# Linear attention and two FFNs on one core: another order of the first FFN's slots, its first sum in two parts, and z written over r

## The chip, the core and the metric

The kernel runs on one core of a Trainium2 chip. The metric is the device time of one execution in microseconds (us), as the median of several runs; lower is better. The core's engines are TensorE (PE, whose weight loads are listed apart as PEld), VectorE (DVE), ScalarE (ACT), GpSimd (POOL) and SyncE (SP), which issues most DMA transfers. The "granted clock" is the share of full speed that the chip allowed TensorE; its two levels are 1.2 and 2.4 GHz.

## The reference

```python
# r, k, v, w: (4, 8, 768, 48); u: (8, 48)
for t in range(S):
    cur = einsum('bhd,bhe->bhde', u * k_t, v_t)
    y[:, :, t] = einsum('bhd,bhde->bhe', r_t, state + cur)
    state = w_t[..., None] * state + einsum('bhd,bhe->bhde', k_t, v_t)
x = y.transpose(0, 2, 1, 3).reshape(3072, 384)
# first FFN, d_ff 2048
h = x @ w_in
x = (h * clip(h + 3, 0, 6) / 6) @ w_out
# second FFN, d_ff 1024
h = x @ w_in2
solu = h * softmax(h)
out = (layernorm(solu) * g_ln) @ w_out2
```

The four FFN weights arrive as 64-bit floats, which the kernel has to turn into pairs of 32-bit numbers itself.

## The kernel before, in words

**Tiles and groups.** The 768 steps of a sequence are cut into 6 groups of 128; a group of the 4 batch entries is 4 tiles, so there are 24 tiles, and tile i belongs to group i // 4. A group is 512 tokens wide (GT), and the first FFN works on whole groups.

**Attention.** A tile passes five stages, `stages = [stw, st0, st1, st2, st3]`. `stw` clamps w on POOL. `st0` transposes w and r on PE into PSUM (wt, rt; from tile 10 on DVE does this from another layout, `late`), and DVE makes running products with eight scans (four into q, four into e) and multiplies e by rt. `st1` transposes k (kt), multiplies q by kt on DVE, and makes z = r*k*u on POOL, in a buffer of its own. `st2` transposes q back (ktp), multiplies q and e on PE into pa0 and pa1, reduces z to d on DVE, and masks on POOL (`am`, a multiplication) and DVE (`am`, a predicated copy from pa0 and pa1). `st3` makes kv and the output yt on PE; DVE adds kv into the state (s_st, twice a tile), ACT copies yt to xh, and DVE makes the remainder xl = yt - xh. All of wt, rt, kt, ktp, pa0, pa1, kv and yt are tiles of one PSUM pool, `ps_a`, with 3 buffers. The state ties tile i to tile i + 4; a group's FFN needs xh and xl of its four tiles.

**The first FFN.** It runs in 96 slots; slot n is (g, m) = divmod(n, 16), chunk m of 128 hidden units for group g. Every product is three matmuls of high and low parts. `ffn_in(n)` runs 9 matmuls into h (2 PSUM buffers), then ACT `t` (L639), DVE `t` (L640), ACT `gh` (L641) and `gl` (L643), on POOL in the first 16 slots and on DVE later. `ffn_out(n - 2)` runs 9 matmuls into the group's three accumulators y (three PSUM banks, one set), in PSUM over all 16 chunks; after the last ACT copies them to `ye` and stores them to `y1d` in DRAM (L661, L662). `xp` holds xh and xl with 2 buffers, and `ye` takes a buffer of xl.

**Weights.** Chunk m of the first FFN's weights is loaded raw by SP (`w1_load`, four DMAs, 2 buffers `raw`), decoded by `w1_a` (DVE L40 and L43, ACT L44) and by `w1_b` (DVE L50 and L53, ACT L60 for w_h, DVE L61 for w_l). L53 is the last to read the raw buffer.

**The order.** A prologue computes the four tiles of group 0 and decodes chunks 0 to 2. Then the program loops over n = 0 to 97: `ffn_in(n)`, the attention stages that the table `sched` puts at n, `ffn_out(n - 2)`, and in slots 0 to 12 the second half of chunk n + 3's decode, the first half of chunk n + 4's and the load of chunk n + 5. Tile i from 4 on has its last stage at slot 4(i - 4) + 2, so tiles 4 to 11 are finished at slots 2, 6, ... 30. In these loops the order of an engine's instructions is arranged by the framework's scheduler, so an engine's rows needn't stand in the order of the program. After slot 78 (NA) the weights of the second FFN are decoded, and after slot 97 the second FFN runs, tile by tile.

Of the kernel before, what the change touches and what calls it, by code (L numbers as in the profile page):

```python
# [8 lines left out]
F32 = mybir.dt.float32  # L9
# [258 lines left out]
def fast_path(  # L268
# [52 lines left out]
    ffp = left.enter_context(tc.tile_pool(name="ff", bufs=3, side="left"))  # L321
    xp = left.enter_context(tc.tile_pool(name="x", bufs=2, side="left"))
    ps_h = left.enter_context(tc.tile_pool(name="ps_h", bufs=2, space=PSUM, side="left"))
# [173 lines left out]
    def st1(i):  # L497
# [20 lines left out]
        nc.vector.tensor_tensor(out=q[0:DP, :, 1:C + 1], in0=kt[0:DP], in1=q[0:DP, :, 1:C + 1], op=ALU.mult)  # L518
        z = atp.tile([P, H, D], F32, tag="z", name="z", bufs=1)
        nc.gpsimd.tensor_tensor(out=z, in0=a["r"][:, :, 0:D], in1=a["k"][:, :, 0:D], op=ALU.mult)  # L520
        nc.gpsimd.tensor_tensor(out=z, in0=z, in1=u_bc, op=ALU.mult)
# [34 lines left out]
    def st3(i):  # L556
# [51 lines left out]
        if b == 0:  # L608
            x_t[g] = (
                xp.tile([P, KD, GT], F32R, tag="xh", name="xh"),  # L610
                xp.tile([P, KD, GT], F32R, tag="xl", name="xl"),
            )
        xh, xl = x_t[g]
# [11 lines left out]
    def ffn_in(n):  # L625
        g, m = divmod(n, M1)
        xh, xl = x_t[g]
# [13 lines left out]
        nc.scalar.activation(out=gh, in_=t, func=ACTF.Copy)  # L641
        eng = nc.gpsimd if n < M1 else nc.vector
        eng.tensor_tensor(out=gl, in0=t, in1=gh.bitcast(F32), op=ALU.subtract)  # L643
        g_t[n] = (gh, gl)

    def ffn_out(n):
        g, m = divmod(n, M1)
        if m == 0:
            y_ps[g] = [ps_y.tile([P, GT], F32, tag=f"y{c}", name=f"y{c}") for c in range(KD)]
        gh, gl = g_t.pop(n)  # L650
        for c in range(KD):
            cs = slice((KD + c) * P, (KD + c + 1) * P)
            wh, wl = w1_h[:, m, cs], w1_l[:, m, cs]
            for j, (a, b) in enumerate([(wh, gh), (wh, gl), (wl, gh)]):
                nc.tensor.matmul(  # L655
                    out=y_ps[g][c], lhsT=a, rhs=b, start=(m == 0 and j == 0), stop=(m == M1 - 1 and j == 2)
                )
        if m == M1 - 1:
            ye = xp.tile([P, KD, GT], F32, tag="xl", name="ye")
            for c in range(KD):  # L660
                nc.scalar.activation(out=ye[:, c, :], in_=y_ps[g][c], func=ACTF.Copy, scale=1.0 / 6.0)  # L661
                nc.scalar.dma_start(out=y1d[g, :, c, :], in_=ye[:, c, :])  # L662
            del y_ps[g]

# [97 lines left out]
    order.close()  # L762
    NA = 4 * (NTILE - B - 1) + 2
    sched = {}
    for i in range(B, NTILE):
        for s in range(NS):
            sched.setdefault(4 * (i - B) + (s - 3 if s < NS - 1 else 2), []).append((i, s))
    for n in sorted(q for q in sched if q < 0):
# [4 lines left out]
    for n in range(NSLOT + LAG):  # L773
# [8 lines left out]
        if n >= LAG:  # L782
            ffn_out(n - LAG)
        if n + LD < M1:
            w1_b(n + LD)
        if n + LD + 1 < M1:
            w1_a(n + LD + 1)
        if n + LD + 2 < M1:
            w1_load(n + LD + 2)
        if n == M1:  # L790
            dec_st.close()
            late_open()
# [125 lines left out]
```

## Time and profile before

| | us |
|---|---|
| runs | 800.91, 800.93, 802.08 (median 800.93) |
| profiled execution | 802.91 |
| its span, first to last instruction | 801.2 |
| mean granted clock of TensorE | 0.970 |
| PE busy in the span | 759.3 (95%) |
| DVE busy | 542.5 (68%) |
| ACT busy | 332.1 (41%) |
| POOL busy | 263.1 (33%) |

The rows further down come from the profiled execution. "Busy" is the time in which an engine has an instruction running. In a row of single instructions the first number is the start and the second the duration in us, and a bracket at the end says how long the engine was idle before it and what ended the wait; "xN" joins N like instructions. L numbers are lines of the kernel before.

### The profile page before, as it was taken

Reading aid. Unit: us, or ns where it says so; the run is one execution under the profiler, and the core shown is the slowest. Engines: PE = TensorE matmul, PEld = TensorE weight load, DVE = VectorE, ACT = ScalarE, POOL = GpSimd, SP = SyncE. Lnnn points to the kernel's source line nnn. Section 1 sums busy time; section 2 is a strip of 40 time slices with the busy share of each in tenths; the row PEclk is TensorE's granted clock in tenths of the full one; section 3 lists DMA queues with packets and bytes.
Section 4 is the critical chain, followed back from the end, with each engine's and each line's share of the span. In section 5 each row is a group of like instructions: output and inputs, shape, how many; then the busy total and the mean of one; then the engine's idle time right before and its main releaser. Section 6 shows DMA issues by size and latency. Waiting matters only on the chain. (4 is left out here: it accounts for less than half of the span.)

```text
span 801.2 us, 13241 instructions
## 1 busy us (share of the span) xinstructions
PE 759.3 (95%) x4922; PEld 639.5 (80%) x4922; DVE 542.5 (68%) x1037; ACT 332.1 (41%) x615; POOL 263.1 (33%) x356
## 2 busy tenths in 40 slices
PE   5788987899999999999999999999999999999996
PEld 4566766688888888888888888877889999999996
DVE  5879789866777776667767665898375555555552
ACT  3355444342334444343344333654353344443342
POOL 5488225573333333333332230232122222222210
PEclk9688889999999999999999999999999999999999
DMA  9964564344333433343323202431111111111001
GB/s 160 174 138 105 130 147 107 86 115 96 82 83 82 121 82 82 83 121 72 73 56 100 52 22 78 138 119 40 50 39 50 41 41 46 44 40 50 29 20 35
DMA packets 139433, 64.76 MB, mean 81 GB/s; under 512 B 90848, under 2 KB 133984, under 8 KB 139360
## 3 DMA queue, kind: packets, MB, share of 16 engines
q1 hardware_dynamic: 136768, 59.11, 31.4%
q10 hardware_dynamic: 2592, 4.72, 1.6%
q8 instruction: 41, 0.67, 0.4%
q14 instruction: 32, 0.26, 0.1%
HBM read 54.37 MB, written 9.44 MB: 80 GB/s over the span
## 5 line engine op out<-in xcount | busy, mean ns | idle before, releaser
L639 ACT ACTIVATE t<-h,three 128x512 f32<-128x512 f32 x96 | 65.8, 685 | 187.0 <-PE h L635 184.4
L635 PE MATMUL h<-xh,w_l 128*128 128x512 f32 x288 | 115.9, 402 | 4.7 <-DVE w_l L61 4.6
L640 DVE SCALAR_TENSOR_TENSOR t<-t,h 128x512 f32<-128x512 f32 x96 | 65.3, 680 | 80.8 <-ACT t L639 80.7
L635 PE MATMUL h<-xh,w_h 128*128 128x512 f32 x288 | 115.3, 401 | 3.6 <-DVE t L640 2.0
L655 PE MATMUL y<-gh,w_h 128*128 128x512 f32 x288 | 117.9, 409 | 0.0
L635 PE MATMUL h<-xl,w_h 128*128 128x512 f32 x288 | 114.9, 399 | 0.0
L655 PE MATMUL y<-gl,w_h 128*128 128x512 f32 x288 | 113.6, 394 | 0.2 <-DVE gl L643 0.2
L655 PE MATMUL y<-gh,w_l 128*128 128x512 f32 x288 | 113.3, 393 | 0.0
L550 POOL TENSOR_TENSOR am<-ident,d 128x512 f32<-128x512 f32 x48 | 59.4, 1259 | 160.3 <-PE yt L585 158.0
L641 ACT ACTIVATE gh<-t 128x512 fp32r<-128x512 f32 x96 | 60.4, 630 | 52.8 <-DVE t L640 51.9
L643 DVE TENSOR_TENSOR gl<-t,gh 128x512 fp32r<-128x512 f32 x80 | 63.9, 798 | 21.8 <-ACT gh L641 21.6
L67 DVE TENSOR_REDUCE nm<-h 128x1 f32<-128x1024 f32 x24 | 29.4, 1225 | 62.6 <-PE h L827 62.5
L635 PEld LDWEIGHTS h<-xh,w_l 128*128 128x128 f32 x288 | 55.8, 194 | 17.9 <-DVE w_l L61 6.4
L635 PEld LDWEIGHTS h<-xh,w_h 128*128 128x128 f32 x288 | 55.2, 192 | 17.3 <-DVE t L640 3.6
L854 PE MATMUL po<-w_oh,qh 128*128 128x384 f32 x192 | 67.0, 349 | 0.3 <-ACT qh L843 0.3
L655 PEld LDWEIGHTS y<-gh,w_h 128*128 128x128 f32 x288 | 54.6, 190 | 15.3 <-ACT gh L641 1.8
L854 PE MATMUL po<-w_oh,ql 128*128 128x384 f32 x192 | 65.2, 339 | 0.1
L854 PE MATMUL po<-w_ol,qh 128*128 128x384 f32 x192 | 65.0, 339 | 0.0
L635 PEld LDWEIGHTS h<-xl,w_h 128*128 128x128 f32 x288 | 55.5, 193 | 11.7
L655 PEld LDWEIGHTS y<-gh,w_l 128*128 128x128 f32 x288 | 54.6, 190 | 12.1
L655 PEld LDWEIGHTS y<-gl,w_h 128*128 128x128 f32 x288 | 54.7, 190 | 11.0 <-DVE gl L643 0.9
L843 ACT ACTIVATE qh<-pt 128x512 fp32r<-128x512 f32 x48 | 26.1, 595 | 79.0 <-PE pt L841 79.0
(118 smaller groups left out, 1515.6 us busy)
## 6 DMA issues: line engine op xcount, KB each, us to landing
raw<-in_moe_w_out_dram SPq DMA_DIRECT2D x24, 384.0 KB
raw<-in_moe_w_in_dram SPq DMA_DIRECT2D x48, 128.0 KB
r<-in_r_dram SPq DMA_DIRECT2D x24, 192.0 KB
k<-in_k_dram SPq DMA_DIRECT2D x24, 192.0 KB
v<-in_v_dram SPq DMA_DIRECT2D x24, 192.0 KB
y1d<-ye ACTq DMA_DIRECT2D x18, 256.0 KB
y<-y1d SPq DMA_DIRECT2D x24, 192.0 KB
out_dram<-os SPq DMA_DIRECT2D x24, 192.0 KB
```

What stands on the lines that cost most here:

```text
L67: nc.vector.tensor_reduce(out=nm, in_=h, axis=AX.X, op=ALU.max, negate=True)
L550: nc.gpsimd.tensor_tensor(out=am, in0=ident.unsqueeze(1).to_broadcast([P, HP, C]), in1=dv[:, hh, :].unsqueeze(2).to_broadcast([P, HP, C]), ...
L635: nc.tensor.matmul(out=h, lhsT=a, rhs=b, start=(j == 0), stop=(j == len(ops) - 1))
L639: nc.scalar.activation(out=t, in_=h, func=ACTF.Relu, bias=three)
L640: nc.vector.scalar_tensor_tensor(out=t, in0=t, scalar=6.0, in1=h, op0=ALU.min, op1=ALU.mult)
L641: nc.scalar.activation(out=gh, in_=t, func=ACTF.Copy)
L643: eng.tensor_tensor(out=gl, in0=t, in1=gh.bitcast(F32), op=ALU.subtract)
L655: nc.tensor.matmul(out=y_ps[g][c], lhsT=a, rhs=b, start=(m == 0 and j == 0), stop=(m == M1 - 1 and j == 2))
L843: nc.scalar.activation(out=qh[:, ms, :], in_=pt, func=ACTF.Copy)
L854: nc.tensor.matmul(out=po, lhsT=x[:, m, :], rhs=y[:, m, :], start=(n == 0), stop=(n == 3 * M2 - 1))
```

## The change

The slots are listed in an order of their own: chunks 0 to 5 of group 0, then all 16 chunks of group 1, then chunks 6 to 15 of group 0, then groups 2 to 5 as before. So group 1 begins at slot 6, and its tiles 4 to 7 have their last stage at slots -1, 1, 3 and 5 (the first in the prologue); group 2 begins at slot 32 as before, and its tiles 8 to 11 end at slots 24, 26, 28 and 30. From tile 12 on the table is the same. Decodes of chunks 3 to 8 follow in slots 0 to 5, those of 9 to 15 in slots 6, 8, ... 18. Since there is one set of accumulators, group 0's sum leaves PSUM after its sixth chunk, by three ACT copies to `part`, and at its end three DVE operations add `part` to the rest. The buffers of x are named a and b in place of two turns of one name, so that group 0's stay while group 1 runs. `gl` stays on POOL up to slot 19, the `late` pool opens at slot 20 in place of 16, and z is written over r.

```diff
+    K0 = 6
+    DEC_END = 20
+    slots = [(0, m) for m in range(K0)] + [(1, m) for m in range(M1)] + [(0, m) for m in range(K0, M1)]
+    slots += [(g, m) for g in range(2, NG) for m in range(M1)]
...
-    xp = left.enter_context(tc.tile_pool(name="x", bufs=2, side="left"))
+    xp = left.enter_context(tc.tile_pool(name="x", bufs=1, side="left"))
+    part_st = ExitStack()
+    part = part_st.enter_context(tc.tile_pool(name="part", bufs=1, side="left")).tile([P, KD, GT], F32, name="part")
...
+    x_room = "ab" + "ba" * (NG // 2)
...
-        z = atp.tile([P, H, D], F32, tag="z", name="z", bufs=1)
-        nc.gpsimd.tensor_tensor(out=z, in0=a["r"][:, :, 0:D], in1=a["k"][:, :, 0:D], op=ALU.mult)
+        z = a["r"][:, :, 0:D]
+        nc.gpsimd.tensor_tensor(out=z, in0=z, in1=a["k"][:, :, 0:D], op=ALU.mult)
...
     def ffn_in(n):
-        g, m = divmod(n, M1)
+        g, m = slots[n]
...
-        eng = nc.gpsimd if n < M1 else nc.vector
+        eng = nc.gpsimd if n < DEC_END else nc.vector
...
     def ffn_out(n):
-        g, m = divmod(n, M1)
-        if m == 0:
+        g, m = slots[n]
+        first = m == 0 or (g == 0 and m == K0)
+        last = m == M1 - 1 or (g == 0 and m == K0 - 1)
+        if first:
...
-        if m == M1 - 1:
-            ye = xp.tile([P, KD, GT], F32, tag="xl", name="ye")
+        if not last:
+            return
+        ys = y_ps.pop(g)
+        if m < M1 - 1:
             for c in range(KD):
...
+                nc.scalar.activation(out=part[:, c, :], in_=ys[c], func=ACTF.Copy, scale=1.0 / 6.0)
+            return
+        ye = xp.tile([P, KD, GT], F32, tag="xl" + x_room[g], name="ye")
+        for c in range(KD):
+            if g == 0:
+                nc.vector.scalar_tensor_tensor(
+                    out=ye[:, c, :], in0=ys[c], scalar=1.0 / 6.0, in1=part[:, c, :], op0=ALU.mult, op1=ALU.add
+                )
...
-    NA = 4 * (NTILE - B - 1) + 2
+    final = {}
+    for i in range(B, NTILE):
+        g, b = divmod(i, B)
+        if g == 1:
+            final[i] = [-1, 1, 3, 5][b]
+        elif g == 2:
+            final[i] = [24, 26, 28, 30][b]
+        else:
+            final[i] = (g - 1) * M1 + 4 * b + 2
+    NA = final[NTILE - 1]
...
-            sched.setdefault(4 * (i - B) + (s - 3 if s < NS - 1 else 2), []).append((i, s))
+            back = NS - 1 - s if i // B < 3 or s == NS - 1 else NS - s
+            sched.setdefault(final[i] - back, []).append((i, s))
+    dec_at = {}
+    for m in range(LD, M1):
+        dec_at[m - LD if m < K0 + LD else K0 + 2 * (m - K0 - LD)] = m
...
-        if n + LD < M1:
-            w1_b(n + LD)
-        if n + LD + 1 < M1:
-            w1_a(n + LD + 1)
-        if n + LD + 2 < M1:
-            w1_load(n + LD + 2)
-        if n == M1:
+        if n in dec_at:
+            m = dec_at[n]
+            w1_b(m)
+            if m + 1 < M1:
+                w1_a(m + 1)
+            if m + 2 < M1:
+                w1_load(m + 2)
+        if n == DEC_END:
             dec_st.close()
             late_open()
```

In the changed kernel's rows the attention lines are numbered some 7 higher (L491 and L497 are the scans L484 and L490, L561 is am L554, L611 is s_st L604, L646 is t L640, L501 is the product with rt L494).

How the change moves DVE's instructions is seen at two places. The first is inside a tile of group 1. Before, from the am of tile 5, with the t of slots 5 and 6:

```order
L554 COPY_PREDICATED am<-causal,pa_923 128x512
L61 TENSOR_TENSOR w_l<-dec,w_h 128x768
L554 COPY_PREDICATED am<-causal,pa_924 128x512
L50 SCALAR_TENSOR_TENSOR dec<-dec,raw 128x768
L640 SCALAR_TENSOR_TENSOR t<-t,h 128x512
L53 SCALAR_TENSOR_TENSOR dec<-raw,dec 128x768
L40 TENSOR_SCALAR dec<-raw 128x768
L640 SCALAR_TENSOR_TENSOR t<-t,h 128x512
L43 TENSOR_SCALAR raw<-raw 128x768
L61 TENSOR_TENSOR w_l<-dec,w_h 128x768
L50 SCALAR_TENSOR_TENSOR dec<-dec,raw 128x768
L604 TENSOR_TENSOR s_st_117<-kv,sp 48x4x48
```

After the change, from the am of tile 6, with the t of slot 3 (and the scans and e of tile 7):

```order
L561 COPY_PREDICATED am<-causal,pa_959 128x512
L561 COPY_PREDICATED am<-causal,pa_960 128x512
L491 SCALAR_TENSOR_TENSOR q<-wt,ones 112x128 x4
L53 SCALAR_TENSOR_TENSOR dec<-raw,dec 128x768
L495 RECIPROCAL e<-q 112x4
L40 TENSOR_SCALAR dec<-raw 128x768
L497 SCALAR_TENSOR_TENSOR e<-wt,e,ones 112x127 x4
L61 TENSOR_TENSOR w_l<-dec,w_h 128x768
L501 TENSOR_TENSOR e<-rt,e 112x512
L43 TENSOR_SCALAR raw<-raw 128x768
L646 SCALAR_TENSOR_TENSOR t<-t,h 128x512
```

Before, decode steps and two t stand between a tile's am and its s_st, and the next tile's scans come later still; now the next tile's scans (tile 7) follow the am at once, and one t lies between am and s_st.

The second place is behind the tiles of group 1. Before, from the t of slot 10, with the end of tile 6 and the scans of tile 7 (s_st, xl, q):

```order
L640 SCALAR_TENSOR_TENSOR t<-t,h 128x512
L61 TENSOR_TENSOR w_l<-dec,w_h 128x768
L43 TENSOR_SCALAR raw<-raw 128x768
L604 TENSOR_TENSOR s_st_119<-kv,sp 48x4x48
L50 SCALAR_TENSOR_TENSOR dec<-dec,raw 128x768
L604 TENSOR_TENSOR s_st_119<-kv,sp 48x4x48
L53 SCALAR_TENSOR_TENSOR dec<-raw,dec 128x768
L40 TENSOR_SCALAR dec<-raw 128x768
L617 TENSOR_TENSOR xl<-yt,xh 128x3x128
L61 TENSOR_TENSOR w_l<-dec,w_h 128x768
L43 TENSOR_SCALAR raw<-raw 128x768
L484 SCALAR_TENSOR_TENSOR q<-wt,ones 112x128 x4
```

After the change, from the t of slot 6, the first of group 1:

```order
L646 SCALAR_TENSOR_TENSOR t<-t,h 128x512
L53 SCALAR_TENSOR_TENSOR dec<-raw,dec 128x768
L646 SCALAR_TENSOR_TENSOR t<-t,h 128x512
L40 TENSOR_SCALAR dec<-raw 128x768
L61 TENSOR_TENSOR w_l<-dec,w_h 128x768
L43 TENSOR_SCALAR raw<-raw 128x768
L491 SCALAR_TENSOR_TENSOR q<-wt,ones 112x128
L50 SCALAR_TENSOR_TENSOR dec<-dec,raw 128x768
L646 SCALAR_TENSOR_TENSOR t<-t,h 128x512
L53 SCALAR_TENSOR_TENSOR dec<-raw,dec 128x768
L40 TENSOR_SCALAR dec<-raw 128x768
L491 SCALAR_TENSOR_TENSOR q<-wt,ones 112x128
```

Where before the decode steps of three chunks share the row with a tile, there are now t and decode steps with single scans of tile 8; all decode steps of chunks 8 to 15 stand in this manner ahead of the t of slot 15.

## Rows read from the trace of the kernel before

**Rows 1.** Timeline of DVE: t of slots 0 and 14 (start, duration, then the instruction)

```profile
61.76 0.67 DVE L640 SCALAR_TENSOR_TENSOR t<-t,h 128x512 f32<-128x512 f32 x1
...
160.46 0.67 DVE L640 SCALAR_TENSOR_TENSOR t<-t,h 128x512 f32<-128x512 f32 x1
```

**Rows 2.** Windows: stretch, length, busy PE, PEld, DVE, ACT, POOL, PE clock, DMA share, GB/s

```profile
62.40:161.20 98.80, 84.32 (x584) 66.95 (x586) 86.83 (x131) 44.38 (x74) 48.32 (x47) 0.89 0.45 113
161.20:267.80 106.60, 106.60 (x824) 88.71 (x816) 71.95 (x139) 41.48 (x79) 41.46 (x54) 1.00 0.42 96
```

**Rows 3.** Waits of DVE and PE, 62.4 to 161.2: total us, times, longest us

```profile
DVE dec L40 <- DMA raw<-in_moe_w_out_dram: 8.7, 6, 2.8
DVE am L554 <- POOL am L550: 0.6, 2, 0.3
...
PE rt L439 <- issue: 8.3, 3, 3.0
```

**Rows 4.** Timeline of ACT: t of slots in PE's full stage

```profile
240.78 0.69 ACT L639 ACTIVATE t<-h,three 128x512 f32<-128x512 f32 x1 [3.77 <-PE h L635]
244.86 0.69 ACT L639 ACTIVATE t<-h,three 128x512 f32<-128x512 f32 x1 [2.00 <-PE h L635]
...
261.51 0.69 ACT L639 ACTIVATE t<-h,three 128x512 f32<-128x512 f32 x1 [3.79 <-PE h L635]
```

**Rows 5.** Lines of DVE, 62.4 to 161.2: count, busy us, mean ns, idle before

```profile
L50 DVE SCALAR_TENSOR_TENSOR dec<-dec,raw 128x768 int32<-128x768 int32 x13 | 14.8, 1136 | 0.0
L53 DVE SCALAR_TENSOR_TENSOR dec<-raw,dec 128x768 int32<-128x768 int32 x13 | 14.6, 1123 | 0.0
L61 DVE TENSOR_TENSOR w_l<-dec,w_h 128x768 fp32r<-128x768 f32 x12 | 14.2, 1181 | 1.8 <-ACT w_h L60 1.7
L640 DVE SCALAR_TENSOR_TENSOR t<-t,h 128x512 f32<-128x512 f32 x15 | 10.1, 674 | 0.2 <-ACT t L639 0.2
L40 DVE TENSOR_SCALAR dec<-raw 128x768 f32<-128x768 f32 x12 | 9.3, 779 | 8.8 <-DMA raw<-in_moe_w_out_dram 8.7
L43 DVE TENSOR_SCALAR raw<-raw 128x768 int32<-128x768 int32 x12 | 6.9, 579 | 0.0
L490 DVE TENSOR_TENSOR_SCAN e<-wt,e,ones 112x127 f32<-112x127 f32 x12 | 4.8, 461 | 0.0
L484 DVE TENSOR_TENSOR_SCAN q<-wt,ones 112x128 f32<-112x128 f32 x12 | 4.1, 403 | 0.0
L494 DVE TENSOR_TENSOR e<-rt,e 112x512 f32<-112x512 f32 x4 | 2.7, 681 | 0.0
L604 DVE TENSOR_TENSOR s_st<-kv,sp 48x192 f32<-48x192 f32 x7 | 2.4, 348 | 0.1
L617 DVE TENSOR_TENSOR xl<-yt,xh 128x384 fp32r<-128x384 f32 x3 | 1.7, 558 | 0.1
L539 DVE TENSOR_REDUCE d<-z 128x8 f32<-128x384 f32 x2 | 1.1, 544 | 0.0
L488 DVE RECIPROCAL e<-q 112x4 f32<-112x4 f32 x3 | 0.5, 176 | 0.0
```

**Rows 6.** L61's durations over the span (min/median/max), and POOL's gl, 62.4 to 161.2

```profile
L61 DVE TENSOR_TENSOR w_l<-dec,w_h x16: 932/950/2028, 28.8 to 161.5; 128x768 fp32r<-128x768 f32 x16
...
L643 POOL TENSOR_TENSOR gl<-t,gh 128x512 fp32r<-128x512 f32 x14 | 20.3, 1452 | 29.1 <-ACT gh L641 29.1
```

**Rows 7.** Timeline of DVE and SP's queue: end of L53, load, L40

```profile
129.00 1.18 DVE L53 SCALAR_TENSOR_TENSOR dec<-raw,dec 128x768 int32<-128x768 int32 x1
...
130.21 1.16 SPq L353 DMA_DIRECT2D raw<-in_moe_w_in_dram  x2
...
137.66 0.56 DVE L40 TENSOR_SCALAR dec<-raw 128x768 f32<-128x768 f32 x1 [0.66 <-DMA raw<-in_moe_w_out_dram]
```

**Rows 8.** Timeline of PE behind slot 14's t

```profile
163.54 0.60 PE L439 MATMUL rt<-ident,r 128*112 128x128 f32 x4
...
169.24 0.39 PE L635 MATMUL h<-xh,w_h 128*128 128x512 f32 x1
```

More of the change, by code (lines that the diff above doesn't have):

```diff
@@ L608, in st3 @@
         if b == 0:
[L609 to L612, printed above, removed]
+            x_t[g] = [
+                xp.tile([P, KD, GT], F32R, tag=nm + x_room[g], name=nm) for nm in ("xh", "xl")
+            ]
         xh, xl = x_t[g]
@@ L655, in ffn_out @@
                 nc.tensor.matmul(
-                    out=y_ps[g][c], lhsT=a, rhs=b, start=(m == 0 and j == 0), stop=(m == M1 - 1 and j == 2)
+                    out=y_ps[g][c], lhsT=a, rhs=b, start=(first and j == 0), stop=(last and j == 2)
                 )
-        if m == M1 - 1:
-            ye = xp.tile([P, KD, GT], F32, tag="xl", name="ye")
+        if not last:
+            return
+        ys = y_ps.pop(g)
+        if m < M1 - 1:
             for c in range(KD):
-                nc.scalar.activation(out=ye[:, c, :], in_=y_ps[g][c], func=ACTF.Copy, scale=1.0 / 6.0)
-                nc.scalar.dma_start(out=y1d[g, :, c, :], in_=ye[:, c, :])
-            del y_ps[g]
+                nc.scalar.activation(out=part[:, c, :], in_=ys[c], func=ACTF.Copy, scale=1.0 / 6.0)
[7 more added lines that the diff above has]
+            else:
+                nc.scalar.activation(out=ye[:, c, :], in_=ys[c], func=ACTF.Copy, scale=1.0 / 6.0)
+            nc.scalar.dma_start(out=y1d[g, :, c, :], in_=ye[:, c, :])
+        if g == 0:
+            part_st.close()
     def range_flag():
@@ L762, in fast_path @@
     order.close()
-    NA = 4 * (NTILE - B - 1) + 2
+    final = {}
[5 more added lines that the diff above has]
+            final[i] = [24, 26, 28, 30][b]
+        else:
+            final[i] = (g - 1) * M1 + 4 * b + 2
+    NA = final[NTILE - 1]
     sched = {}
```

## Prediction

> **What bounds the kernel now.** I read the busy time of each engine by stage first, then what DVE and PE wait for in the stage where neither is full, then DVE's operations there. The profiled execution of before took 802.91 us for a span of 801.2 us; the runs have a median of 800.93 us, 2.0 us less, and I carry every difference over to that median unchanged. I cut the first FFN at two DVE operations that exist in both kernels: the t (L640) of slot 0, which ends at 62.43 us, and that of slot 14, which ends at 161.13 us [rows 1]. Between them PE works 84.32 of 98.80 us at a granted clock of 0.89, DVE 86.83; from there to slot 34's t, at 267.8 us, PE works 106.60 of 106.60 us at 1.00 [rows 2]. So up to slot 14 DVE with its waits sets the pace, and after it PE does. DVE's idle time in the first stage is 98.80 - 86.83 = 12.0 us, and 8.7 of it are waits of L40 for raw weights [rows 2, 3]. PE waits 8.3 us in three places for "issue" ahead of rt [rows 3]; rt takes one of the three buffers of ps_a, which wt, rt, kt, ktp, pa0, pa1, kv and yt share, so this is a wait for a buffer that DVE (or ACT) has yet to read.
>
> From tile 12 on both kernels have the same order, so all that the change can win or lose lies ahead of about slot 34. A slot without attention takes PE 4.08 us; four slots and one tile take 20.73 us, so a tile is 20.73 - 4 x 4.08 = 4.4 us of PE [rows 4].
>
> **The change, part by part.** *Until slot 0's t.* The new DVE row has one L50 and one L494 more ahead of it and one L539 less: 1.136 + 0.681 - 0.544 = 1.27 us of nominal durations [rows 5]. DVE operations overlap a little in the trace: the thirteen lines shown add up to 87.2 us and the two left out, q (L518) and am (L554), to 7.8; together they cover 86.83, a factor of 0.914 [rows 2, 5]. I take **+1.2 us**.
>
> *DVE's work from slot 0's t to slot 14's.* Decoding doesn't move out of the way: although the program now asks for one chunk in two slots, the rows of DVE after the change have all sixteen chunks ahead of slot 15's t, as before. Added are eight scans (four L490, four L484), two s_st, one xl, one reduction (and a reciprocal that is shorter than any of these); gone are one L50, one L53 and one L494. That is 4 x 0.461 + 4 x 0.403 + 2 x 0.348 + 0.558 + 0.544 + 0.18 - 1.136 - 1.123 - 0.681 = 2.5 us, times 0.914: **+2.3 us** [rows 5].
>
> *DVE's idle time there.* In the new order tiles 5, 6 and 7 go through DVE within five slots, where each used to have four, and after tile 7 there is no attention but a few scans until slot 15. So I price two legs.
> In the first leg a tile has nothing between its am and the next tile's scans but a decode step or two, so its chain through the three ps_a buffers and POOL is open. Below: 0.6 us, all that DVE waits for POOL's am now. Above: 8.3 us, if PE's three waits ahead of rt pass to DVE whole [rows 3]. I take the middle, 4.4 us, which is also three times one gl on POOL (1.452 us), the operation that POOL most likely has ahead of an am [rows 6]. With one wait for raw weights of 0.7 us [rows 7] the leg idles 5.1 us.
> In the second leg, from tile 7's xl to slot 14's t, the row holds 8 L50, 7 L53, 7 L61, 7 L40, 7 L43, 9 t, 8 scans and a reciprocal, 44.4 us nominal, times 0.914: 40.6 us [rows 5]. The loads give another bound. A raw buffer is refilled when L53 of its chunk ends: L53 ended at 130.18, the load left at 130.21, and L40 of the chunk two further on could start at 137.66, after a wait, 7.4 us later [rows 7]. From there to the end of that chunk's L53 the row has L40, L43, L61, a scan, L50, a t and L53: 5.88 x 0.914 = 5.4 us. Two buffers thus yield two chunks in 12.8 us, or with a scan less 12.4, so 6.3 us a chunk. Seven chunks are 44.1 us; L50 and L53 of chunk 8 stand ahead (+2.1), L53 of chunk 15 stands behind slot 14's t (-1.0): 45.2 us, of which 4.6 are idle. PE needs only 9 x 4.08 = 36.7 us for the nine slots there.
> Both legs idle 9.7 us where before had 12.0: **-2.3 us**. Slot 14's t thus ends at +1.2 + 2.3 - 2.3 = +1.2 us, at 162.3 us.
>
> *What PE has done by then.* Before, when slot 14's t ended at 161.13, PE still had the end of tile 7's yt, tile 8's wt, 27 FFN matmuls and tile 8's rt and kt to do until it came to h of slot 16 at 169.24: 8.1 us behind [rows 8]. After the change tile 7 is over nine slots earlier and PE waits for each t, so h of slot 16 can start when slot 14's t is out. rt and kt of tile 8 (four transposes each, 0.60 by rt's row, 1.2 us) are still to be paid later. **-6.9 us** on a PE that is full until the end of the stage.
>
> *Tiles 8 to 11 in every second slot (24 to 30).* DVE's share in PE's full stage is 71.95 of 106.60, so 14.0 us of each 20.73; eight of its operations there are t and gl of four slots, at 0.67 some 5.4 us, and a tile is 8.6. Two slots and a tile are then 2.7 + 8.6 = 11.3 us of DVE against 2 x 4.08 + 4.4 = 12.6 of PE: PE still sets the pace, but with little room. Below: 0, as before (106.60 of 106.60). Above: 8.3 us, the three rt waits again [rows 2, 3]. I take **+1.4 us**, a sixth, since DVE has room.
>
> *At nothing, while these covers last:* the three copies of group 0's first sum (ACT works 41.48 of 106.60 us; PE has nine h matmuls to do before it writes y again); the sum on DVE in place of ACT (three operations like t, 2 us, in a stage where DVE idles 35 us); four more gl on POOL, which works 41.46 us there [rows 2]; z over r, which frees r after d only, so that its next load leaves some us later and holds up SP's queue behind it: hidden because tiles' loads are two tiles ahead, and priced in the legs by the raw wait if it shows.
>
> Sum: 1.2 + 2.3 - 2.3 - 6.9 + 1.4 = **-4.3 us**: 798.6 us profiled, 796.6 us as a median. With the first leg's bounds the sum runs from -8.1 (5.9 us idle) to -0.4 (13.6 us idle), with those of slots 24 to 30 as well from -9.5 to +6.5.
>
> **A rule weighed against a row.** L61 lasts 932 ns at best, 950 in the middle and 2028 at worst [rows 6]; it reads two SBUF operands, and on POOL gl takes 1.452 us. My sum gives L61 its mean of 1.181, so some 0.25 us of hindrance for each operation. The Trainium skill ("SBUF — State Buffer", section "Who interferes with whom") says that a DVE instruction with two SBUF inputs and a GpSimd instruction that reads SBUF exclude each other for the whole instruction; by it the sum would be near -0.7 us, and the case is D below. The trace fits it in part: L61's worst is 1.08 us over its middle, less than a whole gl.
>
> **The rivals.**
> *B, faster still: no chain wait and no raw wait.* If DVE's rows interleave as well as they did, idle time falls from 12.0 to 0.6 and the sum is -13.4 us (787.5). For it: the am waits are 0.6 us only. Against: 8.7 us of raw waits, the same buffers. Halfway, 792 us, is its middle.
> *C, slower: the three ps_a buffers with a slow clock.* In the first leg PE waits at each rt or kt for DVE, as in the 8.3 us, and the granted clock, 0.89 on average in that stage and 1.00 where PE is full [rows 2], falls to its lower level (1.2 GHz). Then the 4.4 us of PE for a tile become 8.8, and in a leg where tiles follow each other at once that lengthens the chain: three tiles, 13.2 us, of which half lies beside decoding, leave +6.6: -4.3 + 6.6 = +2.3 us (803.2), at most +8.9 (809.8). Against: the first leg has about 50 us and PE's work in it, 6 slots and three tiles, is 38 us. It makes the kernel slower from 4.3 us of extra waiting on, measurably from 5.9: when slot 14's t ends after 168.2 us.
> *D, gl on POOL locks DVE out.* In the second leg nine gl of 1.45 us, 13.1 us, each hold one DVE operation for its whole length; the means already contain 29 x 0.25 = 7.2. DVE's work there grows by 5.9 us, of which between 0 and the 4.6 idle ones absorb: +1.3 to +5.9, middle 3.6: -0.7 us (800.2).
> *E, slots 24 to 30 stall:* half of the three rt waits, 4.2 in place of 1.4: -1.5 us (799.4).
> *F, the change doesn't do what it says:* the spread decodes are put back together on DVE by the order in which instructions end up, which the rows show; it is in the sum already.
>
> **How the numbers follow.** Forecast 0.40, its own range -7.5 to -0.5; B 0.15; C 0.28; D 0.08; E 0.09. A change of 0.2%, 1.6 us, is what a measurement of this kernel can tell from none. Faster by more: 0.33 of the forecast, all of B, 0.02 of D and 0.04 of E: 0.54. Within 0.2%: 0.06, C 0.05, D 0.05, E 0.04: 0.20. Slower: C 0.22 and the ends of the rest: 0.26. The range, 790 to 806 us, takes in B's middle and C to 3 us above its price; it leaves out the far half of B and the far end of C, under 2 in 10.
>
> **What would show each step.** Slot 14's t (slot 8 of group 1) ends at 160 to 165 us; tile 7's xl at about 118; DVE waits of L40 for raw weights of 4 to 6 us, most of them behind tile 7's xl; PE's waits there for h are long, and h of slot 16 follows slot 14's t at once; from then to slot 34's t PE is full but for 1 or 2 us, in some 101 us where before had 106.6. The prediction is wrong if slot 14's t ends past 168, if PE idles in slots 24 to 30 by more than 4 us, or if the stretch from slot 34 to the end, which I take as unchanged, moves by more than 1 us.

## The result, and the profile after

The changed kernel takes 808.34 us (median of 5 runs, 805.39 to 809.17) against 801.45 us for the kernel before beside it: a ratio of 1.0072, 95% interval 1.0052 to 1.0092. It is slower by about 0.7%, where 0.5% faster was forecast. Its profiled execution took 808.34 us for a span of 806.6 us, 5.4 us longer than that of before.

The stretches of the prediction, read again. First the windows of the changed kernel (stretch, length, busy PE, PEld, DVE, ACT, POOL, granted clock of PE, DMA share, GB/s), cut at the end of slot 0's t, of tile 7's xl, of slot 14's t, then around the tiles 8 to 11, and at the end of slot 34's t:

```profile
65.50:118.70 53.20, 44.42 (x449) 34.50 (x447) 49.09 (x87) 22.06 (x43) 33.53 (x39) 0.94 0.48 105
118.70:167.30 48.60, 40.97 (x175) 31.57 (x173) 38.79 (x55) 23.25 (x34) 14.38 (x11) 1.00 0.41 115
167.30:201.60 34.30, 34.23 (x154) 28.10 (x156) 11.14 (x18) 14.44 (x24) 15.85 (x19) 0.95 0.19 43
201.60:260.00 58.40, 55.17 (x495) 44.82 (x492) 50.23 (x95) 20.90 (x42) 28.59 (x35) 0.97 0.50 113
260.00:273.60 13.60, 13.60 (x113) 11.41 (x115) 9.26 (x16) 4.80 (x9) 3.06 (x4) 1.00 0.52 130
273.60:806.60 533.00, 524.40 (x3228) 448.69 (x3219) 338.51 (x673) 221.75 (x406) 138.67 (x189) 1.00 0.23 63
```

Then the marks themselves and what lies behind tile 7's xl, from the timeline of DVE:

```profile
64.87 0.67 DVE L646 SCALAR_TENSOR_TENSOR t<-t,h 128x512 f32<-128x512 f32 x1
...
118.12 0.56 DVE L623 TENSOR_TENSOR xl<-yt,xh 128x384 fp32r<-128x384 f32 x1
118.59 0.95 DVE L50 SCALAR_TENSOR_TENSOR dec<-dec,raw 128x768 int32<-128x768 int32 x1
119.58 0.96 DVE L53 SCALAR_TENSOR_TENSOR dec<-raw,dec 128x768 int32<-128x768 int32 x1
123.98 0.56 DVE L40 TENSOR_SCALAR dec<-raw 128x768 f32<-128x768 f32 x1 [3.45 <-DMA raw<-in_moe_w_out_dram]
124.58 0.56 DVE L43 TENSOR_SCALAR raw<-raw 128x768 int32<-128x768 int32 x1
...
127.19 0.68 DVE L646 SCALAR_TENSOR_TENSOR t<-t,h 128x512 f32<-128x512 f32 x1
...
166.64 0.68 DVE L646 SCALAR_TENSOR_TENSOR t<-t,h 128x512 f32<-128x512 f32 x1
...
272.90 0.67 DVE L646 SCALAR_TENSOR_TENSOR t<-t,h 128x512 f32<-128x512 f32 x1
```

and the waits of DVE and PE from 118.6 to 167.3 us (total us, times, longest):

```profile
DVE dec L40 <- DMA raw<-in_moe_w_out_dram: 9.7, 6, 3.4
...
PE h L641 <- DVE t L646: 5.3, 3, 2.8
```

Set against [rows 1, 2] and the terms of the sum:

| stretch | forecast, us | measured, us |
|---|---|---|
| start to the end of slot 0's t (before 62.43) | 63.6 | 65.54 |
| to the end of tile 7's xl | 53.6 | 53.14 |
| to the end of slot 14's t | 45.2 | 48.64 |
| to the end of slot 34's t (before 106.6) | 101.1 | 106.25 |
| to the end of the span (before 533.5) | 533.5 | 533.0 |

The first leg and the rest behind slot 34 came out within 0.5 us of the forecast, each on the short side. The other three stretches took 1.9, 3.4 and 5.2 us more. Together that is about the distance of 9.7 us between the forecast of -4.3 and the 5.4 us by which the two profiled spans differ.

**The start.** z over r keeps r until DVE has made d. On POOL the memset of the next r now waits for d, and r's load leaves SP's queue with it, at 47.15 us where before it left at 43.02. What stands right behind it leaves some 4 us later too, the weights of chunk 3 among it (49.03 for 45.07); the weights of chunk 4 leave when they did (52.16 for 52.15). POOL, SP's queue and DVE of the changed kernel:

```profile
47.15 0.20 POOL L393 MEMSET r<- 128x128 f32 x1 [1.48 <-DVE d L546]
...
47.15 0.37 SPq L394 DMA_DIRECT2D r<-in_r_dram  x1
...
49.03 1.16 SPq L359 DMA_DIRECT2D raw<-in_moe_w_in_dram  x2
...
59.60 2.30 DVE L40 TENSOR_SCALAR dec<-raw 128x768 f32<-128x768 f32 x1
```

The last row is L40 of chunk 3, which lasted 1.07 us at 55.17 in the kernel before; it now comes 4.4 us later and falls beside POOL's operations. It doesn't wait for the load when it starts: it stands further back in DVE's row, behind tile 4's d and first scan of e where before it stood behind tile 3's xl.

**Slots 6 to 14.** The rows above show it: after tile 7's xl, L50 and L53, DVE has nothing that it may run, since L40 of chunk 9 stands next in its row and waits 3.45 us for a load, and slot 6's t comes behind it and three more decode steps, 9 us after xl. DVE's waits for raw weights in that stretch are 9.7 us; 4.6 us of idle time were forecast.

**Tiles 8 to 11.** PE is idle for 3.2 us from 201.6 to 260 us and its clock is 0.95 and 0.97 in two stretches where it was to be 1.00. The first of them isn't the tiles' doing: the clock fell behind PE's last wait in the stretch before, that for slot 14's t, and was back by 172 us.

```profile
167.38 0.50 PE L641 MATMUL h<-xh,w_h 128*128 128x512 f32 x1 [1.84 <-DVE t L646]
...
168.00:171.00 3.00, 3.00 (x8) 2.34 (x7) 1.85 (x3) 1.63 (x3) 1.86 (x5) 0.50 0.02 5
```

The worst place among the tiles, in the rows of DVE, POOL and PE, and the window of the matmuls that follow:

```profile
211.45 4.62 DVE L649 TENSOR_TENSOR gl<-t,gh 128x512 fp32r<-128x512 f32 x1 [0.70 <-ACT gh L647]
215.99 0.54 DVE L623 TENSOR_TENSOR xl<-yt,xh 128x384 fp32r<-128x384 f32 x1
216.46 0.68 DVE L525 TENSOR_TENSOR q<-kt,q 112x512 f32<-112x512 f32 x1
...
211.32 0.83 POOL L515 TENSOR_TENSOR sp<-s_st,q 112x384 f32<-112x384 f32 x1
212.12 1.01 POOL L528 TENSOR_TENSOR r<-r,u_bc 128x384 f32<-128x384 f32 x1
213.09 2.04 POOL L557 TENSOR_TENSOR am<-ident,d 128x512 f32<-128x512 f32 x2
215.10 0.40 POOL L519 TENSOR_TENSOR sr<-s_st,q 112x128 f32<-112x128 f32 x1
...
217.19 0.60 PE L539 MATMUL ktp<-ident,q 112*128 112x112 f32 x4 [2.00 <-DVE q L525]
217.72 1.16 PE L550 MATMUL pa<-e,q 48*128 48x128 f32 x16
218.81 0.63 PE L663 MATMUL y<-gh,w_h 128*128 128x512 f32 x1
...
219.00:221.50 2.50, 2.50 (x7) 1.92 (x7) 2.50 (x6) 0.00 (x0) 0.72 (x1) 0.51 0.72 141
```

One gl on DVE, which takes 0.69 us elsewhere, lasts 4.62 us, as long as POOL's five operations of tiles 8 and 9 follow each other. xl of tile 8 and q of tile 9 queue behind it, PE idles 2.0 us for q, and its next FFN matmuls last 0.63 us in place of 0.39: the granted clock is 0.51, the lower of the two levels.

The share of each cost can be estimated from the windows. PE's busy time from 167.3 to 273.6 us is 34.23 + 55.17 + 13.60 = 103.0 us, 3.3 less than the stretch. A mean clock of 0.95 over 34.3 us and 0.97 over 58.4 us means that 1.7 and 1.8 us of full-speed work were lost. So PE had 99.5 us of work to do at full clock; 106.6 - 8.1 + 1.2 = 99.7 were forecast. The rest is 3.3 us of idle time, 1.8 us of clock among the tiles and 1.7 us of clock ahead of them.

### The profile page after: what moved, and what is told of

It is laid out like the page before. It is cut to its first block, busy times and chain, and to the rows that moved or that the text cites. A ratio compares the mean times of both kernels' runs of the same rounds, so it can differ in the third digit from the quotient of the medians.

```text
span 806.6 us, 13254 instructions
## 1 busy us (share of the span) xinstructions
PE 757.4 (94%) x4922; PEld 634.7 (79%) x4922; DVE 545.4 (68%) x1036; ACT 332.0 (41%) x615; POOL 268.1 (33%) x360
## 4 chain that ended last, share of the span: by engine, by line
PE 67%; DVE 15%; issue 6%; DMA 5%; POOL 3%; SPq 2%; ACT 2%; DVEq 0%; POOLq 0%; ACTq 0%
PE y L663 16%; PE h L641 15%; PE po L888 12%; PE h L861 12%; DMA raw<-in_moe_w_out_dram 3%; PE pt L875 3%; PE pa L550 2%; DVE dec L50 2%; PE yt L592 2%; DVE e L497 2%; DVE dec L40 2%; DVE dec L53 2%; DMA raw<-in_moe_w_in_dram 2%; PE yt L585 1%; PE kv L570 1%
## 5 line engine op out<-in xcount | busy, mean ns | idle before, releaser
L645 ACT ACTIVATE t<-h,three 128x512 f32<-128x512 f32 x96 | 65.4, 684 | 161.5 <-PE h L641 158.9
L646 DVE SCALAR_TENSOR_TENSOR t<-t,h 128x512 f32<-128x512 f32 x96 | 65.3, 681 | 81.3 <-ACT t L645 81.2
L641 PE MATMUL h<-xh,w_l 128*128 128x512 f32 x288 | 113.3, 393 | 0.0
L649 DVE TENSOR_TENSOR gl<-t,gh 128x512 fp32r<-128x512 f32 x76 | 66.6, 876 | 18.1 <-ACT gh L647 18.0
L67 DVE TENSOR_REDUCE nm<-h 128x1 f32<-128x1024 f32 x24 | 29.4, 1225 | 62.6 <-PE h L861 62.5
L888 PE MATMUL po<-w_oh,ql 128*128 128x384 f32 x192 | 65.2, 339 | 0.1
```

Source lines behind the costliest of these rows:

```text
L67: nc.vector.tensor_reduce(out=nm, in_=h, axis=AX.X, op=ALU.max, negate=True)
L641: nc.tensor.matmul(out=h, lhsT=a, rhs=b, start=(j == 0), stop=(j == len(ops) - 1))
L645: nc.scalar.activation(out=t, in_=h, func=ACTF.Relu, bias=three)
L646: nc.vector.scalar_tensor_tensor(out=t, in0=t, scalar=6.0, in1=h, op0=ALU.min, op1=ALU.mult)
L888: nc.tensor.matmul(out=po, lhsT=x[:, m, :], rhs=y[:, m, :], start=(n == 0), stop=(n == 3 * M2 - 1))
```

## The experiments

All times are medians beside runs of the kernel before on the same chip; the ratio is to those. It is taken over all the runs and isn't that of the two medians (for the change that would be 1.0086), and the medians of the kernel before differ by chip, 801.15 to 801.84 us. So distances between two kernels are given by their ratios, in us of some 801.5; the changed kernel's own ratio is known to 0.2%, 1.6 us. The four columns behind are ends of the t of slots 0, 6, 14 and 34 in the profiled execution, in us.

| run | us | ratio, 95% interval | 0 | 6 | 14 | 34 |
|---|---|---|---|---|---|---|
| before | 801.45 | 1 | 62.4 | 101.0 | 161.1 | 267.7 |
| the change | 808.34 | 1.0072 (1.0052 to 1.0092) | 65.5 | 127.9 | 167.3 | 273.6 |
| e1_spread | 800.90 | 0.9984 (0.9974 to 0.9995) | 65.0 | 128.4 | 159.9 | 269.6 |
| e2_gl32 | 803.87 | 1.0034 (1.0018 to 1.0050) | 65.1 | 126.0 | 165.8 | 268.5 |
| e3_zown | 803.61 | 1.0023 (1.0007 to 1.0040) | 61.7 | 120.8 | 163.6 | 265.3 |
| e4_raw3 | 803.12 | 1.0012 (0.9999 to 1.0025) | 65.2 | 128.7 | 164.5 | 269.5 |
| e5_before_z | 805.89 | 1.0051 (1.0034 to 1.0067) | 63.1 | 103.7 | 163.7 | 270.8 |
| e6_zk | 808.52 | 1.0079 (1.0054 to 1.0104) | 63.8 | 129.0 | 169.4 | 273.3 |
| e7_spread_zk | 806.59 | 1.0048 (1.0027 to 1.0068) | 64.0 | 127.7 | 164.6 | 272.8 |
| e8_spread_zk_gl32 | 807.84 | 1.0067 (1.0043 to 1.0092) | 63.3 | 126.4 | 163.0 | 272.9 |
| e9_spread_zown | 802.14 | 1.0017 (1.0002 to 1.0033) | 61.7 | 123.1 | 161.6 | 268.4 |
| e10_zown_full | 803.86 | 1.0039 (1.0021 to 1.0058) | 61.7 | 122.3 | 165.8 | 267.6 |
| e11_spread_zown_gl32 | 802.32 | 1.0016 (1.0001 to 1.0030) | 62.6 | 122.8 | 161.5 | 266.4 |
| e12_gl_memset | 804.66 | 1.0046 (1.0032 to 1.0060) | 65.0 | 126.8 | 162.9 | 267.1 |
| e13_chain | 798.17 | 0.9951 (0.9936 to 0.9967) | 62.0 | 124.0 | 161.9 | 265.9 |
| e14_chain_zr | 798.49 | 0.9971 (0.9955 to 0.9986) | 65.2 | 122.8 | 157.2 | 262.9 |
| e15_chain_gl32 | 800.10 | 0.9983 (0.9972 to 0.9994) | 62.8 | 123.3 | 160.4 | 266.1 |

Runs of one kernel lie 2.2 to 6.7 us apart, and a profiled execution can stand more than 3 us from its median: e1's was its slowest (804.30 us), e12's its fastest (801.44), and e13's its slowest (801.37).

**Theory 1: the decode row.** `issue_after` queues what is written in its block behind a named instruction of the same engine.

```diff
+            with tc.issue_after(t_at[n].ins) if n >= K0 else ExitStack():
-            w1_b(m)
-            if m + 1 < M1:
-                w1_a(m + 1)
+                w1_b(m)
+                if m + 1 < M1:
+                    w1_a(m + 1)
```

> The changed kernel with one thing more: from slot 6 on, the decode steps that the program puts at a slot are queued on DVE behind that slot's t, so that they stay spread over slots 6 to 18. Theory 1 (the t of slots 6 to 14 stand behind decode steps that wait for raw weights): slots 6 to 21 run at PE's pace of 4.1 us, slot 21's t comes at about 184 us in place of 192.7, DVE's waits of L40 vanish, and since the stalls of slots 22 to 30 stay, the time is 5 to 10 us below the changed kernel (about 800). Rival (PE waits for PSUM buffers and runs at the lower clock): within 2 us of the changed kernel.

Measured 800.90 us, 7 us below the changed kernel and a little below the one before. From slot 6's t to slot 21's it took 60.7 us, 4.05 a slot: PE's pace. DVE's waits ahead of L40 haven't gone as expected (8.9 us), but now t stands ahead of them; PE waits only 2.3 us for t there. Slot 21's t came at 189.1, not 184, since slot 6's t was as late as in the changed kernel. The theory stands; its rival falls.

**The raw buffers.** `tag="raw"` with `bufs=3` in place of 2, and no `part`.

> The changed kernel with three raw buffers in place of two. To make room, part is left out, so the first six chunks are missing from group 0's sum and three ACT copies are gone. Theory 1 in its form 'the turn-around of the raw buffers is the pace of slots 6 to 14': DVE's waits of L40, 9.7 us, fall under 3, slot 14's t comes 5 to 7 us earlier, the time is 4 to 6 us below the changed kernel. If DVE's own work is the pace there: under 1.6 us.

Measured 803.12 us, 5 us below the changed kernel. L40 waits for no load at all from tile 7's xl to slot 14's t; the one wait of DVE there is

```profile
DVE w_l L61 <- ACT w_h L60: 1.6, 1, 1.6
```

Slot 14's t came only 2.8 us earlier than in the changed kernel, as tile 7 was 2 us later; from slot 6's t to slot 14's it took 35.8 us for 39.4. So the turn-around of the raw buffers is the wait of slots 6 to 14. Without it DVE's own row is not far behind, since slot 14's t was expected 5 to 7 us earlier.

**Theory 3: z over r.** Undone, with one bank of `part` (e3), done alone in the kernel before (e5), put over k (e6), undone with the whole of `part` kept in DRAM (e10):

```diff
-        z = a["r"][:, :, 0:D]
-        nc.gpsimd.tensor_tensor(out=z, in0=z, in1=a["k"][:, :, 0:D], op=ALU.mult)
+        z = atp.tile([P, H, D], F32, tag="z", name="z", bufs=1)
+        nc.gpsimd.tensor_tensor(out=z, in0=a["r"][:, :, 0:D], in1=a["k"][:, :, 0:D], op=ALU.mult)
```

> The changed kernel with z in a buffer of its own again. To make room, part keeps one of its three banks, so two thirds of group 0's first sum are left out and the three copies go to one place. Rival theory 3 (z over r keeps r until DVE's d, so the next r comes late and POOL's operations pile up): POOL's waits for r's load in slots 22 to 30, 7.8 us, fall under 2, the gl of 4.6 us goes, the time is 2 to 4 us below the changed kernel. Theories 1 and 2: within 1.6 us of it.

> The changed kernel with z in a buffer of its own and the whole of part by way of DRAM (the earlier run with z of its own left two thirds of part out). Theory 3: 802 to 805, as that run; slot 0's t at 62 us. If leaving part out was what made that run faster: 807 to 809, as the changed kernel.

> The kernel before with one part of the change alone: z over r. Theory 3, in the form that the run with z in a buffer of its own suggests (r's next load leaves only after d, and every load behind it on SP's queue, weights among them, leaves as much later): slot 0's t at 64.5 to 65.5 us in place of 62.4, the time 2 to 3 us above the kernel before. Rival (in the old order tiles are four slots apart, the loads have time): slot 0's t within 1 us, the time within 1 us.

> The changed kernel with z written over k in place of r, complete. k is loaded behind r and first needed one stage later. Theory 3: slot 0's t at 62 to 63 us in place of 65.5, the time 3 to 5 us below the changed kernel, as with z in a buffer of its own (803.6). Rival (whichever of the two is kept, the queue stands still as long): within 1.6 us of the changed kernel.

e3 and e10 are alike, 803.61 and 803.86, by the ratios 3.9 and 2.6 us below the changed kernel (the interval of e10 overlaps the changed kernel's): leaving `part` out is not the cause. In e3 r's load left at 41.73 us and chunk 3's weights at 43.91, and in both kernels slot 0's t ended at 61.7, 3.8 us earlier:

```profile
41.73 0.37 SPq L394 DMA_DIRECT2D r<-in_r_dram  x1
...
43.91 1.57 SPq L359 DMA_DIRECT2D raw<-in_moe_w_in_dram  x2
```

Of these 3.8 us, 3.0 (e3) and 1.5 us (e10) are left at tile 7's xl (115.65 and 117.23 us for 118.68), and the second leg takes 48.0 and 48.5 us for 48.6, so z over r has no part in that leg. The larger gain comes behind it: from slot 14's t to slot 34's they take 101.7 and 101.8 us for 106.25, where 101.1 were forecast. The windows from slot 23's t to slot 31's, of the changed kernel and then of e10, and e10's longest gl on DVE:

```profile
202.20:260.00 57.80, 54.57 (x485) 44.34 (x484) 49.63 (x95) 20.54 (x41) 28.57 (x34) 0.97 0.50 112
...
200.10:254.00 53.90, 52.05 (x480) 42.82 (x480) 45.56 (x93) 19.09 (x38) 26.10 (x31) 1.00 0.55 122
...
208.32 2.12 DVE L651 TENSOR_TENSOR gl<-t,gh 128x512 fp32r<-128x512 f32 x1 [0.70 <-ACT gh L649]
```

The hold is shorter, PE idles 1.9 us in place of 3.2, and the clock stays at 1.00. POOL's waits for r's load, 7.8 us in the changed kernel, are gone, but POOL waits for k's load instead (4.0 us in e3, 6.1 in e10), so it isn't these waits alone. The other traces agree on the size: from slot 23's t to slot 34's, the six kernels with z of its own take 67.4 to 69.2 us, the changed kernel 71.3, and all nine of the new order with z over r or k 69.4 to 72.5.

Alone in the kernel before, z over r costs 0.5%, 4 us. It does so in another place than expected: slot 0's t is only 0.6 us later, but DVE's waits for raw weights up to slot 14's t grow from 8.7 us [rows 3] to

```profile
DVE dec L40 <- DMA raw<-in_moe_w_out_dram: 12.8, 9, 2.9
```

So the rival, that tiles four slots apart give the loads time, falls. z over k brought nothing, against what I expected: r's load left at 46.15 us there, hardly earlier, right behind POOL's product, which reads r, now also waits for kt's transposes, and ended at 46.12.

**Theory 2: gl on DVE in slots 20 to 31.** `eng = nc.gpsimd if n < 32 else nc.vector`, on the changed kernel, then beside the spread decode steps with z over k (e7, e8), with z of its own (e9, e11) and in the last version (e13, e15).

> The changed kernel with gl on POOL up to slot 31 in place of 19. Theory 2 (in slots 22 to 30 DVE sets the pace: a tile in two slots, gl, and one gl of 4.6 us held up by POOL): from slot 23's t to slot 31's t 51 to 53 us in place of 57.8, the time 4 to 6 us below the changed kernel. Rival (the stall there is PE's: buffers of ps_a and the clock): 0 to 1 us below. Second rival (POOL, with gl and the tiles' own operations, becomes the bound there): not faster or slower.

> The changed kernel with z over k, and with the decode steps of chunks 8 to 15 queued on DVE behind the t of slots 6, 7, 9, 11, 13, 15, 17 and 19. If theories 1 and 3 are two separate costs they add: slot 0's t at 62 to 63, slot 6's t 4 to 5 us behind tile 7's xl, slots 6 to 21 at 4.1 us, slot 21's t at 182 to 185 us, the time 793 to 798. If they are one cost seen twice: 799 to 802, as with the spread alone.

> As the run before it, with gl on POOL up to slot 31. Theory 2 (gl on DVE is part of the stall in slots 22 to 30): 1.5 to 3 us below the run before it, 791 to 796; from slot 23's t to slot 31's t 51 to 54 us. Rival (POOL's gl delays POOL's am and with it the tiles, which are what is waited for there): within 1 us of it or slower.

> The complete version with spread decode steps and z of its own, and gl on POOL up to slot 31. Theory 2 (gl on DVE is part of the stall in slots 22 to 30): 1.5 to 3 us below the version with gl on DVE. Rival (POOL's am comes later behind gl, and the tiles are what is waited for): the same within 1 us or slower, as with z over k.

> The first of these three with gl on POOL up to slot 31. Theory 2: 1.5 to 3 us below it, from slot 23's t to slot 31's t at most 53 us. After two runs in which this moved nothing beside a spread decode (with z over k and with z of its own), the rival is the likelier: within 1 us.

e2 is 3.0 us below the changed kernel, less than theory 2 has it, and its trace bears the theory out only in part: from slot 23's t to slot 31's it took 55.9 us for 57.8, where 51 to 53 were expected, and 1.6 us of its lead are there at slot 14's t already, where DVE's rows of the two kernels are the same. In the three other pairs gl on POOL gained nothing (806.59 and 807.84, 802.14 and 802.32, 798.17 and 800.10). By this one pair of traces the long gl may cost the changed kernel up to 2 us, but gl's engine is no cost of its own. And e7, with z over k and the chunks from 8 on decoded one slot later, is 5.1 us above e1. Since z over k cures nothing (e6), this says nothing on whether theories 1 and 3 add; no run tells which of e7's two differences costs it.

**POOL's reads.** gl of slots 6 to 19 as `nc.gpsimd.memset(gl.bitcast(F32), 0.0)`.

> The changed kernel with gl of slots 6 to 19 as a memset on POOL in place of the subtraction: POOL still writes the buffer at the same place but reads nothing (the low part of the activations is left out there). If POOL's reads of SBUF are what holds single DVE operations (2.05 us for one w_l, 2.02 for one raw, 1.66 for one dec in slots 6 to 14, 4.0 us in all): none of them above 1.3 us from tile 7's xl to slot 14's t, slot 14's t 2 to 4 us earlier. If it is the raw loads alone: durations as before only in part, slot 14's t within 1.5 us.

Measured 804.66 us, by the ratios 2.1 us below the changed kernel, with intervals that overlap: the time alone doesn't show a gain. In the trace, that of the fastest run, the second leg took 44.8 us for 48.6 and slot 14's t ended 4.4 us earlier. The longest L61 (min/median/max in ns) and the operations of DVE and POOL beside each other, after the change and in this run:

```profile
L61 DVE TENSOR_TENSOR w_l<-dec,w_h x16: 929/951/2051, 29.4 to 169.1; 128x768 fp32r<-128x768 f32 x16
...
130.27 2.05 DVE L61 TENSOR_TENSOR w_l<-dec,w_h 128x768 fp32r<-128x768 f32 x1
...
130.22 1.29 POOL L649 TENSOR_TENSOR gl<-t,gh 128x512 fp32r<-128x512 f32 x1 [0.30 <-ACT gh L647]
```

```profile
L61 DVE TENSOR_TENSOR w_l<-dec,w_h x16: 928/950/1248, 29.4 to 164.7; 128x768 fp32r<-128x768 f32 x16
...
136.21 0.95 DVE L61 TENSOR_TENSOR w_l<-dec,w_h 128x768 fp32r<-128x768 f32 x1
...
136.76 0.53 POOL L650 MEMSET gl<- 128x512 f32 x1 [3.55 <-PE y L666]
```

L61, 0.95 us in the median, reached 2.05 us with the subtraction and 1.25 us without, and this 1.25 us fell beside POOL's product sp, which reads too. A memset on POOL in the same place (0.53 us) holds nothing up; a subtraction does. The memset is also shorter than gl by 0.76 us and lets PE's y start earlier, so a part of the shorter leg may be that.

**The order pays when two rows are mended.** The cures of theories 1 and 3 together, with the whole of `part` kept in DRAM, first gave little:

> A complete version: the changed kernel with the decode steps of chunks 8 to 15 queued on DVE behind the t of slots 6, 7, 9, 11, 13, 15, 17 and 19, and with z in a buffer of its own. The room for z comes from part, which goes to DRAM bank by bank through two small buffers and is loaded back into the free xh of group 0 before slot 32. If the decode row (theory 1) and z over r (theory 3) are separate costs: slot 0's t at 62, slot 21's t at 182 to 185 us, the time 791 to 797, clearly below both kernels. If they overlap: 799 to 802.

802.14 us: no sum of two gains. Its DVE and SP rows show why. L40 of the next chunk stands ahead of L53, and L53 is what frees the buffer for the load after, so every chunk takes a whole load:

```profile
144.61 1.09 DVE L50 SCALAR_TENSOR_TENSOR dec<-dec,raw 128x768 int32<-128x768 int32 x1
148.95 0.56 DVE L40 TENSOR_SCALAR dec<-raw 128x768 f32<-128x768 f32 x1 [3.25 <-DMA raw<-in_moe_w_out_dram]
149.43 0.95 DVE L53 SCALAR_TENSOR_TENSOR dec<-raw,dec 128x768 int32<-128x768 int32 x1
...
141.39 1.16 SPq L361 DMA_DIRECT2D raw<-in_moe_w_in_dram  x2
...
150.40 1.16 SPq L361 DMA_DIRECT2D raw<-in_moe_w_in_dram  x2
...
159.19 1.16 SPq L361 DMA_DIRECT2D raw<-in_moe_w_in_dram  x2
```

The loads leave 9.0 and 8.8 us apart, and two slots of PE take 8.2. In e13 and e14 the first half of the next chunk's decode is queued behind L53 (`LAST` is that instruction), and, as in e9, every chunk from 8 on is decoded one slot later than in the change. e13 has z of its own and also holds the stages of tiles 8 to 11 behind t, so that slot 6's t doesn't wait for tile 8's d (4.3 us in e9); e14 keeps z over r and `part` as the change has them.

```diff
+            with tc.issue_after(t_at[n].ins) if n >= K0 else ExitStack():
+                w1_b(m)
             if m + 1 < M1:
+                with tc.issue_after(LAST[0].ins) if n >= K0 else ExitStack():
+                    w1_a(m + 1)
```

> The complete version with spread decode steps and z of its own, with two orders on DVE mended: the first half of chunk m+1's decode (L40) is queued behind the last of chunk m (L53), which frees the raw buffer, where L40 stood ahead of L53 and so made each chunk wait for a whole load (7.4 us and two operations, 8.9 us a chunk against 8.2 us for two slots of PE); and the stages of tiles 8 to 11 are queued behind the t of the slot before, so that slot 6's t no longer waits 4.3 us behind tile 8's d. Theory 1 (the raw turn-around is what is left of the cost in slots 6 to 14): slot 6's t 4 to 5 us behind tile 7's xl, from slot 6's t to slot 14's 32 to 34 us in place of 38.5, slot 34's t at 258 to 262 us, the time 792 to 797. Rival (the gain of the slot order is used up elsewhere, by PE's own work and the clock): 800 to 803, as without.

> The same order of decode steps (without that of the tiles' stages), with z over r as in the changed kernel and part in SBUF. If z over r costs 4 us beside the decode row: 4 us above the complete version with z of its own. If its cost is only that of late raw loads, which now have time: within 1.6 us of it.

Both beat both kernels: 798.17 us (0.9951) and 798.49 us (0.9971). Two windows of e14, tile 7's xl to slot 14's t and on to slot 21's, and DVE's xl of tile 7 and t of slot 6:

```profile
118.30:157.20 38.90, 37.65 (x167) 30.86 (x166) 29.71 (x35) 19.96 (x30) 10.38 (x8) 1.00 0.38 106
157.20:182.80 25.60, 25.40 (x117) 20.79 (x116) 19.03 (x23) 12.65 (x19) 9.41 (x14) 1.00 0.27 75
```

```profile
117.76 0.56 DVE L626 TENSOR_TENSOR xl<-yt,xh 128x384 fp32r<-128x384 f32 x1
122.08 0.69 DVE L650 SCALAR_TENSOR_TENSOR t<-t,h 128x512 f32<-128x512 f32 x1 [3.77 <-ACT t L649]
```

Slot 6's t stands right behind xl; PE works 37.65 of 38.90 and 25.40 of 25.60 us at a clock of 1.00; slot 14's t ends at 157.2 us, 10 us before the changed kernel's. In e13's profiled execution, its slowest, one wait of 4.5 us for raw weights and a clock of 0.92 from tile 7's xl on kept slot 14's t to 161.9, so its range of marks was missed though its time was only 1 us over. With decode steps in this order z over r costs no more than can be told (0.9951 and 0.9971, intervals that overlap), though e14 takes 70.5 us from slot 23's t to slot 34's and e13 67.7.

## Why the prediction was wrong, by its steps

- **z over r at nothing** is the step that failed most: "hidden because tiles' loads are two tiles ahead". I had seen that SP's queue stands still behind r; the load of the weights behind it has no such cover, and the sum had no term for it among tiles 8 to 11 either. It shows in two places.
- **The t of slot 0 at +1.2 us** measured +3.1. With z of its own it ends at 61.7 us, ahead of the kernel before, and L50 and the product with rt stand behind it again (e3, e10): the 1.2 us that I counted came from z over r too.
- **Tiles 8 to 11 at +1.4 us** measured 6.7, so rival E, at 4.2, was still too small. With z of its own the stretch takes 101.7 and 101.8 us in place of 106.25, near the 101.1 of the forecast. That DVE had room (11.3 of 12.6 us) was true on average, but one gl held for 4.62 us used up the room of two tiles, and I had no term for the clock that falls behind a gap in PE. In all, z over r costs 4 us alone (e5), and undone it gives back 3.9 and 2.6 us (e3, e10).
- **DVE's work and the first leg** were right: 53.14 us for 53.6. Tiles 5 to 7 waited little, at a clock of 0.94. So rival C had the sign, and its price (803.2) was nearer than the forecast, but its mechanism, PSUM buffers and a slow clock in the first leg, is not what happened.
- **The second leg, 45.2 us,** was mis-sized: 48.64. DVE worked 38.8 us there, 1.8 less than forecast, and idled 9.8, not 4.6. I let the two raw buffers start in full swing; but the last chunks of the first leg are late, so that the leg opens with a wait of 3.45 us (load out at 115.68), and L50, L61 and L43 beside POOL's gl (up to 2.05 us) stretch the turn. Three buffers remove the wait (e4).
- **Case D** was real as a mechanism: beside a memset no L61 is held as it is beside gl (e12). The Trainium skill ("SBUF — State Buffer", section "Who interferes with whom") says that a DVE instruction with two SBUF inputs contends with a GpSimd instruction that reads SBUF, and not with one that only writes it; e12 agrees, with 0.95 us beside a memset and 2.05 beside a subtraction. I had given the case a chance of 0.08 and a price of 3.6 us, in one stretch only; holds of this kind also made L40 2.30 us at the start and gl 4.62 us among tiles 8 and 9.
- **The credit of 6.9 us** was right: PE had an estimated 99.5 us of work left for 99.7 forecast.
- **Rival F** I took as nothing, "in the sum already". So it was, as far as the forecast goes; but it was the largest lever. Putting the decode steps where the program asks for them gave 7 us (e1), and 8 to 10 with the row in the right order (e14, e13). The sum had their work, but not that a t, which PE waits for, stands in the row behind a step that waits for a load.

None of the three signs that I had named showed: slot 14's t ended at 167.3 us, ahead of 168, PE idled 3.2 us in slots 24 to 30, and the rest behind slot 34 moved by 0.5 us. The errors added up below them.

Open: why the tiles 8 to 11 pass more slowly with z over r, as POOL waits for a load either way; and the 1.7 us of clock at 168 us, which the traces of e2, e4, e6, e10 and e12 don't have (1.00 from slot 14's t to slot 23's).

## What to carry to other kernels

When a change asks for work in other slots, read the order in which each engine finally gets its instructions, and look for an operation that waits for a load ahead of one that another engine waits for; pinning a few such places turned a loss of 0.7% into a gain of 0.3 to 0.5%. A buffer that is reused to save room is paid where its next load stands in a queue: price every load behind it, for every tile that passes there. Where two engines' operations exclude each other, price the longest row of back-to-back operations, not a mean.

## What the runs showed of the hardware

A DVE operation with two SBUF operands was held while four to six operations of POOL that read SBUF ran one behind another: 4.62 us in place of 0.69 here, 5.21 and 4.57 us in e1 and e4, and 4.23 in e12, where only earlier gl were changed. In e12, L61 beside a memset of POOL lasted its usual 0.95 us. DVE operations with one tensor operand were held as well beside POOL's operations (L40 2.30 us for 0.56, L43 2.02 for 0.55). Gaps of 2.00 and 1.84 us in PE's row were followed by stretches of 2.5 and 3 us at a granted clock of 0.51 and 0.50, with matmuls of 0.63 us where 0.39 is usual.
